# A decay-gated attention layer and a mixer MLP in one kernel: the recurrence, the loads and the order of all work rebuilt

## The chip, the core and the metric

One core of a Trainium2 chip runs the whole program. The metric is the device time of one execution in microseconds (us); lower is better. TensorE is called PE in the profile, VectorE DVE, ScalarE ACT, GpSimd POOL and SyncE SP.

## What is computed

Inputs: q, k, v, alpha of shape (4 batches, 8 heads, 768 steps, 48), float32, and the mixer's U (768 x 32), V (32 x 768), w_ch1 (384 x 1536), w_ch2 (1536 x 384). The output is (4, 768, 384) float32.

```python
state = np.zeros((B, H, D, D))
for t in range(S):
    state = alpha[:, :, t, :, None] * state + np.einsum('bhd,bhe->bhde', k[:, :, t], v[:, :, t])
    y[:, :, t] = np.einsum('bhd,bhde->bhe', q[:, :, t], state)
x = y.transpose(0, 2, 1, 3).reshape(B, S, H * D)
h = x.transpose(0, 2, 1) @ U @ V
u = x + h.transpose(0, 2, 1)
out = u + np.maximum(u @ w_ch1, 0.0) @ w_ch2
```

## The kernel before

A batch's 768 steps are cut into six chunks of 128; there are 24 chunks. `gla_chunk` does one. It loads alpha, q and k as float32 on the SP queue (lines 105 to 110; four buffers each) and v, cast to bf16 on its way, on the POOL queue (line 111). Ln of alpha (line 116) goes through two triangular matmuls: one gives the running sum from the chunk's start (line 119), one the sum from a step to the chunk's end (line 122). Three Exps turn these into `a_sb`, `ainv` and `arev` (lines 125 to 132). POOL makes q times `a_sb` (line 134) and k times `arev` (line 137), DVE makes k times `ainv` (line 135). PE transposes the q and k products, two heads at a time (lines 141 and 145), and DVE and ACT copy them to `qkT` (lines 150, 151). Scores of the even and odd heads (line 159) are masked by DVE (line 166). The chunk's y is the part from the state (line 173, two heads per matmul) plus the part from the scores (line 180), and ACT copies it to `x_b` (line 186). The state that a chunk hands on is made from its own k and v alone (line 191) and copied by DVE (lines 198, 199): decay over a whole chunk of 128 steps is so strong that what an older chunk leaves is dropped.

`moe_part(b, i)` is the mixer of a batch in six parts. Part 0 makes U^T x (line 208), V^T of that (line 216), u (line 220) and u transposed (lines 230, 242). Parts 1 and 2 are the MLP's first layer for one half of the steps each: 12 groups of three matmuls of 384 columns (line 251), with Relu on ACT and DVE in turn (lines 258, 262). Parts 3 to 5 are the second layer: 12 matmuls for each chunk (line 270), the add of u (line 277) and the store on the SP queue (line 278).

The order is that of the loop at the end: chunk c of batch b, then part c of the mixer of batch b - 1; the weights are sent on the POOL queue after the first chunk, 15 transfers with a cast to bf16, then U and V (lines 75 to 79). A scheduler of the language's library puts the engines' instructions in order and adds all waits. PSUM is eight banks: two for the sums, one for transposes, two and one for scores and state, and two (`pgen`) that y, the mixer and both MLP layers share.

Of the kernel before, what the change touches and what calls it, by code (L numbers as in the profile page):

```python
# [11 lines left out]
ALU = mybir.AluOpType  # L13


@with_exitstack
def kernel(
# [25 lines left out]
    xb_pool = ctx.enter_context(tc.tile_pool(name="xb_pool", bufs=2))
    io = ctx.enter_context(tc.tile_pool(name="io", bufs=4))
    work = ctx.enter_context(tc.tile_pool(name="work", bufs=4))
    moes = ctx.enter_context(tc.tile_pool(name="moes", bufs=2))
    outp = ctx.enter_context(tc.tile_pool(name="outp", bufs=4))

    pcum = ctx.enter_context(tc.tile_pool(name="pcum", bufs=2, space=bass.MemoryType.PSUM))
    ptp = ctx.enter_context(tc.tile_pool(name="ptp", bufs=1, space=bass.MemoryType.PSUM))  # L50
    ppts = ctx.enter_context(tc.tile_pool(name="ppts", bufs=2, space=bass.MemoryType.PSUM))
    ptodd = ctx.enter_context(tc.tile_pool(name="ptodd", bufs=1, space=bass.MemoryType.PSUM))
    pgen = ctx.enter_context(tc.tile_pool(name="pgen", bufs=2, space=bass.MemoryType.PSUM))

    def bank(pool, dtype=FP32, name="bk"):
        cols = 512 if dtype == FP32 else 1024
        return pool.tile([128, cols], dtype, name=name, tag="bk")
# [32 lines left out]
    ring_s = const.tile([128, 3, HP, 2 * D], BF16)  # L90
    nc.vector.memset(ring_s, 0.0)

    def pslice(ring, slot, p, wid=W):
        return ring[:, slot].rearrange("t h w -> t (h w)")[
            :, 2 * p * 64 : 2 * p * 64 + wid
        ]

    xs = [None] * B
    us = [None] * B

    def gla_chunk(b, c):
        x_b = xs[b]
        sl = slice(c * C, (c + 1) * C)
        slot = (b * NC + c) % RING
        at = io.tile([C, H, D], FP32, name="at")
        nc.sync.dma_start(at, alpha[b, :, sl, :].rearrange("h t d -> t h d"))
        qt = io.tile([C, H, D], FP32, name="qt")
        nc.sync.dma_start(qt, q[b, :, sl, :].rearrange("h t d -> t h d"))
        kt = io.tile([C, H, D], FP32, name="kt")
        nc.sync.dma_start(kt, k[b, :, sl, :].rearrange("h t d -> t h d"))  # L110
        nc.gpsimd.dma_start(  # L111
            ring_v[:, slot, :, 0:D], v[b, :, sl, :].rearrange("h t d -> t h d")
        )

        lt = work.tile([C, H * D], BF16, name="lt")
        nc.scalar.activation(lt, at.rearrange("t h d -> t (h d)"), AF.Ln)  # L116

        cum_ps = bank(pcum)[:, : H * D]
        nc.tensor.matmul(cum_ps, lhsT=ut_ones, rhs=lt, start=True, stop=True)  # L119
        if c < NC - 1:  # L120
            rev_ps = bank(pcum)[:, : H * D]
            nc.tensor.matmul(rev_ps, lhsT=sl_ones, rhs=lt, start=True, stop=True)

        a_sb = work.tile([C, H, D], BF16, name="a_sb")
        nc.scalar.activation(a_sb.rearrange("t h d -> t (h d)"), cum_ps, AF.Exp)  # L125
        ainv = work.tile([C, H, D], BF16, name="ainv")
        nc.scalar.activation(  # L127
            ainv.rearrange("t h d -> t (h d)"), cum_ps, AF.Exp, scale=-1.0
        )
        if c < NC - 1:  # L130
            arev = work.tile([C, H, D], BF16, name="arev")
            nc.scalar.activation(arev.rearrange("t h d -> t (h d)"), rev_ps, AF.Exp)  # L132

        nc.gpsimd.tensor_tensor(ring_q[:, slot, :, 0:D], qt, a_sb, op=ALU.mult)  # L134
        nc.vector.tensor_tensor(ring_k[:, slot, :, 0:D], kt, ainv, op=ALU.mult)  # L135
        if c < NC - 1:
            nc.gpsimd.tensor_tensor(ring_kh[:, slot, :, 0:D], kt, arev, op=ALU.mult)  # L137

        tp_ps = bank(ptp, BF16).rearrange("p (e c) -> p e c", c=C)
        for p in range(HP):  # L140
            nc.tensor.matmul(  # L141
                tp_ps[0:W, p, :], lhsT=pslice(ring_q, slot, p), rhs=ident,
                start=(p == 0), stop=False, is_transpose=True,
            )
            nc.tensor.matmul(  # L145
                tp_ps[0:W, HP + p, :], lhsT=pslice(ring_k, slot, p), rhs=ident,
                start=False, stop=(p == HP - 1), is_transpose=True,
            )
        qkT = work.tile([128, 8, C], BF16, name="qkT")
        nc.vector.tensor_copy(qkT[0:W, 0:HP], tp_ps[0:W, 0:HP])  # L150
        nc.scalar.copy(qkT[0:W, HP:], tp_ps[0:W, HP:])  # L151

        ptm = work.tile([C, H, C], BF16, name="ptm")
        pt_e = bank(ppts).rearrange("p (hp c) -> p hp c", c=C)
        pt_o = bank(ptodd).rearrange("p (hp c) -> p hp c", c=C)
        for par, pt_ps in ((0, pt_e), (1, pt_o)):
# [126 lines left out]
    for b in range(B + 1):  # L283
# [40 lines left out]
```

## Time and profile before

| | |
|---|---|
| median of 3 timed runs | 279.08 us (277.88 to 280.98) |
| span of the profiled execution, first to last instruction | 275.9 us |
| busy in it: PE / DVE / ACT / POOL | 197.0 / 132.0 / 137.1 / 75.1 us |
| mean granted clock of PE | 0.893 |
| read from HBM, written to HBM | 23.79 MB, 4.72 MB |

The profiled execution is told by its span; what lies around the span is seen only in the timed runs, whose median is 3.2 us above it. Busy time of PE has a modelled end for each matmul, so that overlapping matmuls are counted as one stretch and a single one is longer than its turn; the spacing of starts is the measure of a turn. An L and a number is a line of the kernel; `idle before` is how long the engine stood still ahead of a group, with what ended it.

### The profile page before, as it was taken

Reading aid. Unit: us, or ns where it says so; the run is one execution under the profiler, and the core shown is the slowest. Engines: PE = TensorE matmul, PEld = TensorE weight load, DVE = VectorE, ACT = ScalarE, POOL = GpSimd, SP = SyncE. Lnnn points to the kernel's source line nnn. Section 1 sums busy time; section 2 is a strip of 40 time slices with the busy share of each in tenths; the row PEclk is TensorE's granted clock in tenths of the full one; section 3 lists DMA queues with packets and bytes.
Section 4 is the critical chain, followed back from the end, with each engine's and each line's share of the span. In section 5 each row is a group of like instructions: output and inputs, shape, how many; then the busy total and the mean of one; then the engine's idle time right before and its main releaser. Section 6 shows DMA issues by size and latency. Waiting matters only on the chain.

```text
span 275.9 us, 3982 instructions
## 1 busy us (share of the span) xinstructions
PE 197.0 (71%) x1492; PEld 113.5 (41%) x1492; DVE 132.0 (48%) x247; ACT 137.1 (50%) x230; POOL 75.1 (27%) x99
## 2 busy tenths in 40 slices
PE   1440144856877878789627999987599998779995
PEld 0220023644244445445215556653455564344462
DVE  1330124664546545358515777458558644544421
ACT  3990789489889785555972553012034401014300
POOL 5736943564112034043101344242110000000000
PEclk9999999995557999999755999999579999959999
DMA  8999999999705594876502452435020011100022
GB/s 134 189 198 198 165 150 197 159 200 147 98 0 103 56 147 80 146 132 96 75 0 56 47 71 37 74 93 55 2 14 2 0 59 57 57 0 2 0 86 87
DMA packets 106306, 23.94 MB, mean 87 GB/s; under 512 B 101264, under 2 KB 105904, under 8 KB 106288
## 3 DMA queue, kind: packets, MB, share of 16 engines
q1 hardware_dynamic: 78336, 18.88, 32.2%
q0 software_dynamic: 27952, 4.82, 21.9%
q8 instruction: 11, 0.18, 0.2%
q14 instruction: 7, 0.06, 0.1%
HBM read 23.79 MB, written 4.72 MB: 103 GB/s over the span
## 4 chain that ended last, share of the span: by engine, by line
PE 50%; ACT 24%; issue 9%; DVE 8%; DMA 7%; SPq 1%; POOL 0%; ACTq 0%; DVEq 0%; POOLq 0%
PE bk L270 17%; PE bk L251 15%; DMA at<-in_alpha_dram 7%; ACT L116 5%; ACT L125 4%; PE bk L159 4%; ACT a_sb L125 3%; ACT ainv L127 2%; ACT lt L116 2%; ACT qkT L151 2%; PE bk L191 2%; PE bk L119 2%; ACT arev L132 2%; PE bk L141 2%; DVE h1t L262 2%
## 5 line engine op out<-in xcount | busy, mean ns | idle before, releaser
L251 PE MATMUL bk<-uT,w_sb 128*128 128x384 bf16 x288 | 61.4, 344 | 6.6 <-ACT h1t L258 3.7
L270 PE MATMUL bk<-w_sb,h1t 128*128 128x384 bf16 x288 | 51.3, 326 | 0.9 <-ACT x_b L186 0.4
L166 DVE TENSOR_TENSOR ptm<-bk,maskc 128x512 bf16<-128x512 f32 x48 | 31.5, 686 | 34.4 <-PE bk L159 33.9
L258 ACT ACTIVATE h1t<-bk 128x384 bf16<-128x384 f32 x48 | 23.6, 492 | 34.6 <-PE bk L251 32.7
L119 PE MATMUL bk<-lt,ut_ones 128*128 128x384 bf16 x24 | 10.3, 436 | 40.4 <-ACT lt L116 29.1
L251 PEld LDWEIGHTS <-w_sb 128*128 128x128 bf16 x288 | 27.8, 102 | 27.4 <-issue 14.1
L262 DVE TENSOR_SCALAR h1t<-bk 128x384 bf16<-128x384 f32 x48 | 26.7, 557 | 23.7 <-PE bk L251 23.0
L134 POOL TENSOR_TENSOR ring_q<-qt,a_sb 128x384 bf16<-128x384 f32 x24 | 22.4, 934 | 51.9 <-PE bk L145 23.1
L270 PEld LDWEIGHTS <-h1t 128*128 128x128 bf16 x288 | 26.8, 98 | 17.5 <-issue 1.2
L135 DVE TENSOR_TENSOR ring_k<-kt,ainv 128x384 bf16<-128x384 f32 x24 | 20.4, 855 | 25.0 <-ACT ainv L127 16.8
L111 POOL DMA_DIRECT2D ring_v<-in_v_dram x24 | 22.6, 941 | 28.6 <-PE bk L180 21.9
L137 POOL TENSOR_TENSOR ring_kh<-kt,arev 128x384 bf16<-128x384 f32 x20 | 18.6, 928 | 41.8 <-issue 20.0
L116 ACT ACT_TABLE_LOAD x19 | 24.4, 1283 | 9.2 <-DMA at<-in_alpha_dram 8.1
L277 DVE TENSOR_TENSOR out_sb<-u_b,bk 128x384 f32<-128x384 bf16 x24 | 13.3, 554 | 30.7 <-PE bk L270 30.7
L125 ACT ACT_TABLE_LOAD x17 | 21.8, 1283 | 10.8 <-PE bk L119 10.6
L186 ACT CAST x_b<-bk 128x384 bf16<-128x384 f32 x24 | 11.5, 479 | 29.0 <-PE bk L180 28.9
L151 ACT COPY qkT<-bk 112x512 bf16<-112x512 bf16 x24 | 14.1, 587 | 19.5 <-DVE qkT L150 19.2
L159 PE MATMUL bk<-qkT 48*128 48x128 bf16 x192 | 15.2, 252 | 9.0 <-ACT qkT L151 8.6
L141 PE MATMUL bk<-ident,ring_q 128*112 128x128 bf16 x96 | 19.1, 263 | 1.9 <-DVE uT L242 1.9
L145 PE MATMUL bk<-ident,ring_k 128*112 128x128 bf16 x96 | 19.3, 262 | 0.1
L141 PEld LDWEIGHTS <-ring_q 128*112 128x112 bf16 x96 | 15.6, 168 | 6.2 <-POOL ring_kh L137 4.6
L159 PEld LDWEIGHTS <-qkT 48*128 48x128 bf16 x192 | 8.0, 106 | 24.2 <-ACT qkT L151 18.1
(48 smaller groups left out, 230.9 us busy)
## 6 DMA issues: line engine op xcount, KB each, us to landing
at<-in_alpha_dram SPq DMA_DIRECT2D x24, 192.0 KB, 4.2
qt<-in_q_dram SPq DMA_DIRECT2D x24, 192.0 KB, 3.8
kt<-in_k_dram SPq DMA_DIRECT2D x24, 192.0 KB, 3.6
out_dram<-out_sb SPq DMA_DIRECT2D x24, 192.0 KB, 1.8
ring_v<-in_v_dram POOLq DMA_DIRECT2D x24, 96.0 KB, 3.8
w_sb<-in_moe_w_ch_dram POOLq DMA_DIRECT2D x3, 384.0 KB, 8.2
w_sb<-in_moe_w_ch_dram POOLq DMA_DIRECT2D x12, 96.0 KB, 7.2
u_sb<-in_moe_U_dram POOLq DMA_DIRECT2D x1, 48.0 KB, 6.7
```

Of the source, the lines that this page charges most:

```text
L111: nc.gpsimd.dma_start(ring_v[:, slot, :, 0:D], v[b, :, sl, :].rearrange("h t d -> t h d"))
L116: nc.scalar.activation(lt, at.rearrange("t h d -> t (h d)"), AF.Ln)
L125: nc.scalar.activation(a_sb.rearrange("t h d -> t (h d)"), cum_ps, AF.Exp)
L134: nc.gpsimd.tensor_tensor(ring_q[:, slot, :, 0:D], qt, a_sb, op=ALU.mult)
L135: nc.vector.tensor_tensor(ring_k[:, slot, :, 0:D], kt, ainv, op=ALU.mult)
L141: nc.tensor.matmul(tp_ps[0:W, p, :], lhsT=pslice(ring_q, slot, p), rhs=ident, start=(p == 0), stop=False, is_transpose=True,)
L159: nc.tensor.matmul(pt_ps[:, p, :], lhsT=qkT[o : o + D, HP + p, :], rhs=qkT[o : o + D, p, :], start=(p == 0), stop=(p == HP - 1),)
L166: nc.vector.tensor_tensor(ptv, pt_ps, maskc.to_broadcast([C, HP, C]), op=ALU.mult)
L251: nc.tensor.matmul(h1_ps, lhsT=w1_sb[:, ct, jt * 128 : (jt + 1) * 128], rhs=uT[:, ct, tt * TW : (tt + 1) * TW], start=(ct == 0), stop=(ct ...
L258: nc.scalar.activation(h1t[:, jt, tt * TW : (tt + 1) * TW], h1_ps, AF.Relu)
L262: nc.vector.tensor_scalar_max(h1t[:, jt, tt * TW : (tt + 1) * TW], h1_ps, 0.0)
L270: nc.tensor.matmul(ch_ps, lhsT=h1t[:, jt, c * C : (c + 1) * C], rhs=w2_sb[:, jt, :], start=(jt == 0), stop=(jt == NJ - 1),)
```

## The change

Both functions are rewritten, and all work is put into a list of operations with an engine, a cost in ns, what is read and written, and a priority. A planner in the kernel (`Plan`) walks through the list at build time: it keeps a clock for each engine and a line for the loads, takes always the operation that can start first, by priority where several can, gives it buffers and PSUM banks, and then emits everything in that order, which the library keeps (`manual_schedule`).

- All four inputs of a chunk are loaded as float32 on the SP queue, in the order alpha, k, q, v, into a ring of 40 tiles (ten chunks). POOL casts v to bf16.
- One sum from the chunk's start is left. Four matmuls with one column add the chunk's totals; a small Exp makes `tot` of them. The sum to the chunk's end, its Exp and the third product are gone.
- The state is kept in full: the old state is added through a matmul with the identity, k and v products of 48 columns are added to it, and DVE multiplies the sum by `tot`. The state part of y is one matmul of 48 rows per head.
- Both products are on POOL. The copies of u transposed move from DVE to ACT.
- The set of activation tables with Ln and Exp is named at the start.
- U and V (V four times) are sent after chunk 0, the first weight, as one transfer, after x of chunk 3, the second after x of chunk 4. U^T x is made in four strips of 32 rows.
- PSUM: two pairs of banks for scores and y, two banks for sums, transposes, state and mix, two for the MLP; the last batch's MLP takes any.
- Chunks have priority over the MLP, the mix over both.

The new code, cut to its core (the old code stands above):

```diff
+    LAT = {"PE": 230.0, "ACT": 120.0, "DVE": 120.0, "POOL": 150.0, "SP": 0.0, "DMA": 0.0}
...
+            for eng, cand in ready.items():
+                now = clock.get(eng, 0.0)
+                ok = []
+                for op in cand:
+                    t = op.est
+                    for b in op.bufs:
+                        if b.slot is None:
+                            s = [x for p in b.pools for x in p.free if x is not None]
+                            if not s:
+                                t = None
+                                break
+                            t = max(t, min(s))
+                    if t is not None:
+                        ok.append((max(t, now), op))
+                if not ok:
+                    continue
+                t0 = min(t for t, _ in ok)
+                t1, op = min(((t, o) for t, o in ok if t <= t0 + 1.0), key=lambda x: (x[1].prio, x[1].i))
+                if best is None or t1 < best[0]:
+                    best = (t1, eng, op)
...
+            if eng == "SP":
+                clock[eng] = t + 450.0
+                dma = max(dma, t + 450.0) + op.cost
+                op.end = dma + 1800.0
+            else:
+                clock[eng] = t + op.cost
+                op.end = t + op.cost
...
+        for _, op in order:
+            op.fn()
...
+def mm(*cols):
+    return sum(max(c, 54) / 2.4 + 2.5 for c in cols)
...
+    nc.scalar.preload_act_table_set("natural_log_exp_and_others")
...
+    io = Pool(slots("io", 40, [C, H, D], FP32))
...
+    outs = Pool(slots("ou", 4, [C, DM], FP32))
...
+    ps = psum.tile([128, 8, 512], FP32, name="ps")
+    pair = Pool([ps[:, 0:2, :], ps[:, 2:4, :]])
+    gen = Pool([ps[:, 4, :], ps[:, 5, :]])
+    mlp = Pool([ps[:, 6, :], ps[:, 7, :]])
...
+    def load_w1():
+        nc.gpsimd.dma_start(w1_sb, moe_w_ch1.rearrange("(c p) f -> p c f", p=128))
+    def load_w2():
+        nc.gpsimd.dma_start(w2_sb, moe_w_ch2.rearrange("(c p) f -> p c f", p=128))
...
+        at, qt, kt, vt = (Buf(io) for _ in range(4))
+        for t, src in ((at, alpha), (kt, k), (qt, q), (vt, v)):
+            P.add("SP", 960, lambda t=t, src=src: nc.sync.dma_start(t(), src[b, :, sl, :].rearrange("h t d -> t h d")), w=[t], prio=kk)
+        lt = Buf(lts)
+        P.add("ACT", 510, lambda: nc.scalar.activation(lt()[:, :, 0:D], at(), AF.Ln), r=[at], w=[lt], prio=pr + 4)
+        rv = Buf(rvs)
+        P.add("POOL", 500, lambda: nc.gpsimd.tensor_copy(rv(), vt()), r=[vt], w=[rv], prio=pr + 5)
...
+        def f_cum():
+            nc.tensor.matmul(cb()[:, 0:DM], lhsT=ut_ones, rhs=lt()[:, :, 0:D], start=True, stop=False)
+            for p in range(HP):
+                nc.tensor.matmul(
+                    cb()[:, DM + p : DM + p + 1],
+                    lhsT=lt()[:, 2 * p : 2 * p + 2, :].rearrange("t h w -> t (h w)"),
+                    rhs=ones, start=False, stop=(p == HP - 1),
+                )
+        P.add("PE", mm(DM, 1, 1, 1, 1), f_cum, r=[lt], w=[cb], prio=pr + 3, after=[done.get(kk - 2)])
...
+        P.add("ACT", 490, lambda: nc.scalar.activation(ai().rearrange("t h d -> t (h d)"), cb()[:, 0:DM], AF.Exp, scale=-1.0), r=[cb], w=[ai], prio=pr + 2)
+        P.add("ACT", 490, lambda: nc.scalar.activation(aa().rearrange("t h d -> t (h d)"), cb()[:, 0:DM], AF.Exp), r=[cb], w=[aa], prio=pr + 2)
+        P.add("ACT", 200, lambda: nc.scalar.activation(tot()[:, :, 0], cb()[:, DM : DM + HP], AF.Exp), r=[cb], w=[tot], prio=pr + 2)
...
+        P.add("POOL", 930, lambda: nc.gpsimd.tensor_tensor(rk()[:, :, 0:D], kt(), ai(), op=ALU.mult), r=[kt, ai], w=[rk], prio=pr + 2)
+        P.add("POOL", 930, lambda: nc.gpsimd.tensor_tensor(rq()[:, :, 0:D], qt(), aa(), op=ALU.mult), r=[qt, aa], w=[rq], prio=pr + 2)
...
+        P.add("PE", 220, lambda: f_tr(rk, HP), r=[rk], w=[(tb, "k")], prio=pr + 2, after=[done.get(kk - 2)])
+        P.add("PE", 220, lambda: f_tr(rq, 0), r=[rq], w=[(tb, "q")], prio=pr + 2)
+        P.add("ACT", 590, lambda: f_qk(HP, "ACT"), r=[(tb, "k"), (tb, "q")], w=[(qk, "k")], prio=pr + 1)
+        P.add("DVE", 410, lambda: f_qk(0, "DVE"), r=[(tb, "q"), (tb, "k")], w=[(qk, "q")], prio=pr + 1)
...
+        P.add("PE", mm(*[C] * 4) * 1.2, f_sc, r=[(qk, "k"), (qk, "q")], w=[sc], prio=pr + 1)
...
+            P.add("DVE", 690, lambda par=par: f_mask(par), r=[sc], w=[(pm, par)], prio=pr + 1)
...
+        def f_y(par):
+            y2 = yb()[:, par, 0 : HP * D].rearrange("p (hp d) -> p hp d", d=D)
             o = 64 * par
             for p in range(HP):
+                if sprev is not None:
+                    nc.tensor.matmul(
+                        y2[:, p, :], lhsT=qk()[o : o + D, p, :],
+                        rhs=sprev()[o : o + D, p, :], start=(p == 0), stop=False,
+                    )
             for p in range(HP):
                 nc.tensor.matmul(
+                    y2[:, p, :], lhsT=pm()[:, 2 * p + par, :], rhs=rv()[:, 2 * p + par, :],
+                    start=(p == 0 and sprev is None), stop=(p == HP - 1),
...
+            P.add("PE", mm(*[D] * 8), lambda par=par: f_y(par), r=rs + [(pm, par)], w=[(yb, par)], prio=pr)
...
+        P.add("ACT", 520, f_x, r=[(yb, 0), (yb, 1)], w=[(xb, c)], prio=pr)
...
+            def f_d():
+                d2 = db()[:, 0 : HP * D]
+                sp = sprev() if sprev is not None else s_zero
+                nc.tensor.matmul(d2[0:W], lhsT=ident[0:W, 0:W], rhs=sp[0:W].rearrange("p a d -> p (a d)"), start=True, stop=False, skip_group_check=True)
+                d3 = d2.rearrange("p (hp d) -> p hp d", d=D)
+                for p in range(HP):
+                    for par in range(2):
+                        o = 64 * par
+                        nc.tensor.matmul(
+                            d3[o : o + D, p, :], lhsT=rk()[:, 2 * p + par, 0:D], rhs=rv()[:, 2 * p + par, :],
+                            start=False, stop=(p == HP - 1), skip_group_check=True,
...
+            P.add("PE", mm(HP * D, *[D] * 8), f_d, r=[rk, rv] + ([sprev] if sprev is not None else []), w=[db], prio=pr + 1)
+            P.add(
+                "DVE", 340,
+                lambda: nc.vector.tensor_tensor(
+                    st()[0:W], db()[0:W, 0 : HP * D].rearrange("p (hp d) -> p hp d", d=D),
+                    tot()[0:W].to_broadcast([W, HP, D]), op=ALU.mult,
+                ),
+                r=[db, tot], w=[st], prio=pr,
...
+        P.add("PE", mm(DM) * 1.4, lambda: f_utx(range(0, 4)), r=[(xb, c) for c in range(4)] + ["u"], w=[xu], prio=pr)
+        P.add("PE", mm(DM) * 1.2, lambda: f_utx(range(4, NC)), r=[(xb, c) for c in range(4, NC)] + ["u"], w=[xu], prio=pr)
+        utx = Buf(utxs)
+        P.add("ACT", 490, lambda: nc.scalar.copy(utx(), xu()[:, 0:DM]), r=[xu], w=[utx], prio=pr)
...
+                P.add("ACT", 830, f_ev, r=[ub2], w=[(uT, c // 2)], prio=pr)
...
+        pool = [mlp] if b < B - 1 else [mlp, gen, pair]
...
+            if jt % 2 == 0:
+                P.add("ACT", 500, lambda jt=jt, hb=hb: nc.scalar.activation(h1()[:, jt, tt * TW : (tt + 1) * TW], bank(hb)[:, 0:TW], AF.Relu), r=[hb], w=[(h1, tt, jt)], prio=100)
+            else:
+                P.add("DVE", 560, lambda jt=jt, hb=hb: nc.vector.tensor_scalar_max(h1()[:, jt, tt * TW : (tt + 1) * TW], bank(hb)[:, 0:TW], 0.0), r=[hb], w=[(h1, tt, jt)], prio=100)
...
+        hb = Buf([mlp] if b < B - 1 else [mlp, gen, pair])
+        pr = 5000 + b * 1000 + 100 + (c % 3) * 33 + (0 if c < 3 else 100)
...
+            P.add("PE", mm(*[DM] * 4), f, r=[(h1, tt, jt) for jt in range(4 * g, 4 * g + 4)] + ["w2"], w=[hb], prio=pr + g)
+        ou = Buf(outs)
+        P.add("DVE", 550, lambda: nc.vector.tensor_tensor(ou(), ub()[:, c, :], bank(hb)[:, 0:DM], op=ALU.add), r=[hb, (ub, c)], w=[ou], prio=100)
+        P.add("SP", 550, lambda: nc.sync.dma_start(out[b, c * C : (c + 1) * C, :], ou()), r=[ou], prio=-1)
...
+            if b == 0 and c == 3:
+                x = P.ops[-1]
+                P.add("POOL", 1000, load_w1, r=[(xb, c)], w=["w1"], prio=0)
+            if b == 0 and c == 4:
+                P.add("POOL", 1000, load_w2, r=[(xb, c)], w=["w2"], prio=0)
...
```

## Rows read from the trace of the kernel before

**Rows 1.** The page: span, busy time of the engines, and the chain by engine.

```profile
span 275.9 us, 3982 instructions
...
PE 197.0 (71%) x1492; PEld 113.5 (41%) x1492; DVE 132.0 (48%) x247; ACT 137.1 (50%) x230; POOL 75.1 (27%) x99
...
PE 50%; ACT 24%; issue 9%; DVE 8%; DMA 7%; SPq 1%; POOL 0%; ACTq 0%; DVEq 0%; POOLq 0%
```

**Rows 2.** Busy time by stretch; the first line names the columns.

```profile
core 0: us, PE busy (x) PEld busy (x) DVE busy (x) ACT busy (x) POOL busy (x), PEclk, DMA share, GB/s
...
12.00:34.00 22.00, 4.50 (x30) 2.28 (x30) 3.56 (x7) 13.11 (x21) 15.34 (x24) 1.00 1.26 185
...
63.00:87.00 24.00, 17.84 (x118) 9.52 (x117) 12.08 (x25) 20.80 (x31) 5.03 (x7) 0.50 0.59 90
...
203.00:240.00 37.00, 34.04 (x283) 19.65 (x282) 20.42 (x40) 10.36 (x21) 0.94 (x1) 1.00 0.14 35
```

**Rows 3.** MLP matmuls: duration ns min/median/max, first and last start in us.

```profile
L251 PE MATMUL bk<-uT,w_sb x288: 322/326/528, 81.9 to 260.5; 128*128 128x384 bf16 x144
L270 PE MATMUL bk<-w_sb,h1t x288: 322/326/337, 109.0 to 272.2; 128*128 128x384 bf16 x144
```

**Rows 4.** Groups by line: busy us, mean ns, idle before and its releasers.

```profile
L116 ACT ACT_TABLE_LOAD x19 | 24.4, 1283 | 9.2 <-DMA at<-in_alpha_dram 8.1 <-PEq L308 0.8
...
L125 ACT ACT_TABLE_LOAD x17 | 21.8, 1283 | 10.8 <-PE bk L119 10.6
L134 POOL TENSOR_TENSOR ring_q<-qt,a_sb 128x384 bf16<-128x384 f32 x24 | 22.4, 934 | 51.9 <-PE bk L145 23.1 <-issue 14.6 <-ACT lt L116 5.2
...
L135 DVE TENSOR_TENSOR ring_k<-kt,ainv 128x384 bf16<-128x384 f32 x24 | 20.4, 855 | 25.0 <-ACT ainv L127 16.8 <-DMA kt<-in_k_dram 8.2
...
L151 ACT COPY qkT<-bk 112x512 bf16<-112x512 bf16 x24 | 14.1, 587 | 19.5 <-DVE qkT L150 19.2
...
L132 ACT ACTIVATE arev<-bk 128x384 bf16<-128x384 f32 x20 | 10.1, 505 | 1.2 <-PE bk L122 1.2
```

**Rows 5.** ACT in order of time: a table load and the Ln behind it.

```profile
33.84 1.28 ACT L116 ACT_TABLE_LOAD   x1
...
35.13 0.52 ACT L116 ACTIVATE lt<-at 128x384 bf16<-128x384 f32 x1
```

**Rows 6.** SP's queue while weights come in: first and last of six loads.

```profile
12.41 5.09 SPq L106 DMA_DIRECT2D at<-in_alpha_dram  x1
...
25.54 7.97 SPq L106 DMA_DIRECT2D at<-in_alpha_dram  x3
```

**Rows 7.** SP's queue without weights: first of nine loads, and the tenth.

```profile
40.42 0.65 SPq L110 DMA_DIRECT2D kt<-in_k_dram  x1
...
50.30 1.30 SPq L108 DMA_DIRECT2D qt<-in_q_dram  x1
```

**Rows 8.** PE in order of time, 202.9 to 208 us: start, length, what.

```profile
202.93 0.22 PE L145 MATMUL bk<-ident,ring_k 128*112 128x128 bf16 x1
202.98 0.22 PE L141 MATMUL bk<-ident,ring_q 128*112 128x128 bf16 x1
...
203.09 0.34 PE L180 MATMUL bk<-ring_v,ptm 128*128 128x48 bf16 x7
...
206.07 1.15 PE L251 MATMUL bk<-uT,w_sb 128*128 128x384 bf16 x6
207.16 0.34 PE L159 MATMUL bk<-qkT 48*128 48x128 bf16 x4
207.43 0.82 PE L251 MATMUL bk<-uT,w_sb 128*128 128x384 bf16 x4
```

**Rows 9.** PE at the end: two of the first layer's pairs of groups, then the second layer.

```profile
253.67 1.14 PE L251 MATMUL bk<-uT,w_sb 128*128 128x384 bf16 x6 [0.16 <-DVE h1t L262]
...
254.97 1.14 PE L251 MATMUL bk<-uT,w_sb 128*128 128x384 bf16 x6 [0.16 <-DVE h1t L262]
...
260.63 11.86 PE L270 MATMUL bk<-w_sb,h1t 128*128 128x384 bf16 x72
```

More of the change, by code (lines that the diff above doesn't have):

```diff
@@ L13, with __init__, __call__ @@
 ALU = mybir.AluOpType
+class Pool:
+    def __init__(self, slots):
+        self.slots = list(slots)
+        self.free = [0.0] * len(self.slots)
+class Buf:
+    def __init__(self, pool=None, slot=None):
+        self.pools = pool if isinstance(pool, list) else ([pool] if pool else [])
+        self.slot = slot
+        self.home = None
+        self.idx = 0
+        self.left = 0
+        self.last = 0.0
+    def __call__(self):
+        return self.slot
+class Op:
+    __slots__ = ("eng", "cost", "fn", "prio", "deps", "bufs", "n", "end", "users", "est", "i", "keep")
@@ L40 @@
     W = 112
+    TW = S // 2
     const = ctx.enter_context(tc.tile_pool(name="const", bufs=1))
[L43 to L57, printed above, removed]
@@ L71, with slots @@
-    vm_sb = const.tile([R, S], BF16)
+    psum = ctx.enter_context(tc.tile_pool(name="psum", bufs=1, space=bass.MemoryType.PSUM))
+    ctx.enter_context(tc.manual_schedule())
+    def slots(name, n, shape, dtype):
+        return [const.tile(shape, dtype, name=f"{name}{i}") for i in range(n)]
+    P = Plan()
+    nc.scalar.preload_act_table_set("natural_log_exp_and_others")
+    ut_ones = const.tile([C, C], BF16, name="ut_ones")
+    make_upper_triangular(nc, ut_ones, val=1.0, diag=True)
+    ident = const.tile([C, C], BF16, name="ident")
@@ L90 @@
[L90 to L102, printed above, removed]
-        sl = slice(c * C, (c + 1) * C)
[L104 to L143, printed above, removed]
-            )
[L145 to L156, printed above, removed]
@@ L270, in moe_part, with bank, mlp2, f @@
+    def bank(hb):
+        x = hb()
+        return x[:, 0, :] if len(x.shape) == 3 else x
+    def mlp2(b, ub, h1, c):
+        hb = Buf([mlp] if b < B - 1 else [mlp, gen, pair])
+        pr = 5000 + b * 1000 + 100 + (c % 3) * 33 + (0 if c < 3 else 100)
+        tt = c // 3
+        for g in range(3):
+            def f(g=g):
+                for jt in range(4 * g, 4 * g + 4):
                     nc.tensor.matmul(
-                        ch_ps,
-                        lhsT=h1t[:, jt, c * C : (c + 1) * C],
@@ L287 @@
+    for b in range(B):
+        xb, ub, uT, h1 = Buf(xbs), Buf(ubs), Buf(uts), Buf(h1s)
+        st = None
         for c in range(NC):
-            if b < B:
-                gla_chunk(b, c)
+            st = stage_gla(b, c, st, xb)
             if b == 0 and c == 0:
-                load_weights()
-            if b > 0:
-                moe_part(b - 1, c)
+                P.add("POOL", 1000, load_weights, w=["u", "vm"], prio=1000 + 25)
+            if b == 0 and c == 3:
[3 more added lines that the diff above has]
+                P.add("POOL", 1000, load_w2, r=[(xb, c)], w=["w2"], prio=0)
+        stage_mix(b, xb, ub, uT)
+        mlp1(b, uT, h1, 0)
+        mlp1(b, uT, h1, 1)
+        for c in range(NC):
+            mlp2(b, ub, h1, c)
```

341 lines of the change are left out of this document (208 added, 133 removed).

## The prediction

> **What bounds the kernel now.** I read the page first. Its totals [rows 1] show no engine that is full: PE, the busiest, is busy 197.0 us of the span of 275.9, and the chain that ended last is only half PE; a quarter of it is ACT and 7% is loads. So the time goes into waits between engines, and the question is where. The stretches [rows 2] say: from 12 to 34 us PE works 4.5 of 22 us while the DMA engines are full (share 1.26 by the profile's account); from 203 to 240 us PE is busy 34 of 37 us. The first and last starts of the MLP matmuls [rows 3] put a date to it: the first one starts at 81.9 us, the last at 272.2. The kernel is thus two parts: 82 us in which six chunks of attention are fetched and the mix is made, and 190 us in which PE does nearly all its matmuls. The groups [rows 4] show a reason for the slow first part and for holes in the second: 36 table loads of 1.28 us (19 before Ln, 17 before Exp) are 46.2 of ACT's 137.1 us, and they stand in the chain of every chunk.
>
> **PE's work, piece by piece, after the change.** At full clock a matmul of 384 columns follows the last one after 0.163 us (72 in 11.7 us, less the modelled end [rows 9]), one of 128 columns (a transpose) after 0.055, one of 48 columns after about 0.025 (seven in 0.34 us, of which some 0.18 is the last one's own latency) [rows 8].
> - MLP, unchanged: 576 x 0.163 = 93.7 us.
> - A chunk: running sum 0.16 and four one-column totals at 0.03; eight transposes 0.44; scores about 0.25; y sixteen of 48 columns 0.4; state one of 192 columns 0.08 and eight of 48 columns 0.2. Together 1.65 us.
> - A change of the array's shape: between two runs of full matmuls the four score matmuls with 48 rows cost more than their columns. Six matmuls from 206.07 should end their turn at 207.05, the scores start at 207.16; and they hold PE 0.27 us where four turns, two side by side, are 0.11 [rows 8]. So one visit costs about 0.2 us. A chunk now has four such visits (scores, two state parts of y, the state's 48-column strips): 0.75 us. The strips have no row of their own; between 0 and 0.2 I take 0.2, as the scores are the nearest.
> - Mix of a batch: six packed matmuls about 0.42, six of 384 columns 0.98, 18 transposes 1.0, visits 0.4: 2.8 us.
> The sum is 93.7 + 24 x 2.4 + 4 x 2.8 = 162.5 us, hardly other than before: the change saves PE no work. The Trainium skill (TensorEngine Tiling (Array Packing), Key Properties) says that a change of tiling mode, not of tile alone, drains TensorE; the scores' row agrees with it at 0.2 us, and by it the strips pay too; if they paid nothing the sum would be 24 x 0.2 = 5 us less.
>
> **When PE can begin.** In the stretch without weight transfers, nine loads of 192 KB go out between 40.42 and 50.30 us [rows 7], 1.1 us each, some v transfers of the other queue among them; I take 1.0 for a load alone. A chunk has now four of them on one queue: 4 us, six chunks 24, the first landing at about 3 us. While the weights came in before, six loads took 21 us (12.41 to 33.5 [rows 6]): the weights cost the loads about 15 us. Now they are sent after x of chunks 3 and 4, at about 25 and 29 us, so they delay chunk 5 little and the loads of the second batch much; with landing times of about 8 us and half of the engines, w1 is there at about 37 us. Chunk 5 lands at 28 to 30 us, x follows 5 us later (two multiplications of 0.93 on POOL, transposes, copies, masks, y), and the mix takes 6 us in its chain of copies. MLP starts at about 41 us instead of 81.9. Bounds: 35 (no delay by weights) and 60 (PE's fixed order has chunks 6 to 8 ahead of the first MLP groups, and their loads land behind the weights; the planner books the weights at 1 us of POOL and nothing on the DMA engines). In these 41 us PE gets seven chunks and a mix done: 7 x 2.4 + 2.8 = 19.6, so 143 us are left.
>
> **From there to the end.** Loads are 96 x 1.0 + 15 for weights, with stores perhaps 120 us, so the last chunk lands at about 120 us, when PE still has some 70 us of MLP to do: loads no longer bound the end, PE does. ACT loses the table loads and the third Exp (46.2 + 10.1), takes the uT copies (12 at about 0.9, from 0.587 for 512 columns [rows 4]) and 24 small Exp: about 95 us of work. DVE loses the k product (20.4): 112. POOL has two products of 0.93 and a cast of v of about 0.5 per chunk: 57. None reaches PE's 162. What PE loses to waits: MLP's first layer of batches 0 to 2 still has two PSUM banks, and where two banks alternated in the last stretch, six matmuls came every 1.30 us [rows 9] against 0.98 of their own. If nothing fills these holes they cost 36 pairs x 0.32 = 11.5 us; chunks, and the second layer's matmuls of the first half, lie beside some of it, so I take 7, no wait saved as the lower end, and as the upper end that PE's second part takes as long as before, 190 us. End of PE: 41 + 143 + 7 = 191. Behind the last matmul stand the add and the store, as before: 275.9 - 272.5 = 3.4. Span 194. The timed runs' median, 279.08, lies 3.2 above the profiled span, and I add as much: **197 us**. Its own range is 183 to 212.
>
> **Tables, by page and by row.** An Ln starts at 35.13 us, 0.01 after the load that began at 33.84 has ended [rows 5]: a switch costs 1.28 us. The Trainium skill (ScalarE: Activation LUTs, What ACT_TABLE_LOAD costs) says 1283 ns and about 1380 ns of drain, 2.66 us for every switch; the trace shows the first part and not the second. The same page (Table sets: the hidden batching unit) has Ln and Exp in one set, which no run here shows yet. By its 2.66 the 36 switches would be 96 us of ACT and not 46; what goes is off the path once PE bounds, so the sum stays.
>
> **Rivals.**
> 1. *The table loads stay* (the preload is not honoured). Then ACT has about 95 + 46 = 141 us, in the chunk phase 3.9 + 2.6 us per chunk: 18 chunks x 6.5 from 33 us end at 150, MLP of two batches and more is left, about 55 us. 150 + 55 + 3.4 + 3.2 = 212. For it: the choice of set is not the kernel's in what I see. Against: both functions can sit in one set.
> 2. *Fixed orders block.* Each engine works through the planner's order, and a late load, weight or store holds all behind it; stores go on the loads' queue behind loads sent far ahead, and only four output buffers exist. PE's second part then takes what it took before: 41 + 190 + 6.6 = 238; half of that loss gives 218.
> 3. *Better than summed*: MLP at 36 us, visits half price (-8), no holes: 36 + 135 + 6.6 = 177.
> 4. *The clock stays low: slower than before.* From 63 to 87 us the granted clock was 0.50, the 1.2 GHz level, though PE was busy 17.8 of 24 us; from 203 to 240 it was 1.00, the 2.4 GHz level, at 34 of 37 [rows 2]. If loads pace PE until 120 us and it is then cut by bank waits, it may stay at the lower level. All of the 143 us at that level gives 41 + 286 + 6.6 = 334; the sign turns when more than 0.55 of the work (79 us) runs there: 41 + 143 + 7 + 79 + 6.6 = 277. Against: MLP filled in leaves few holes.
>
> **How the numbers follow.** Forecast 0.64, rival 1 0.07, rival 2 0.14, rival 3 0.11, rival 4 0.04. The range, 173 to 226, holds rivals 1 and 3 and the milder half of 2; outside are its worse half, rival 4 and errors of a load's price. All but rival 4 and a sliver of 2 are faster by over 1%, which is about what can be told from no change: faster 0.95, same 0.01, slower 0.04.
>
> **What would show it.** Right: one table load; first MLP matmul at 36 to 48 us; loads full until about 120 us; PE's MLP spacing 0.163 and granted clock 1.00 from then on; chain mostly PE (70% or more). Wrong: MLP start beyond 60 us, DVE waiting for store buffers, table loads of more than two, PE idle over a tenth of the time between the first and the last MLP matmul, or the lower clock in more than a quarter of it.

## The result and the profile after

The kernel after takes 212.31 us (median of 4, 211.37 to 212.57) against 279.14 us (277.88 to 280.98): a ratio of 0.762, 95% interval 0.758 to 0.767. The forecast was 197, its range 173 to 226; the sign and the range hold, the time is 15 us longer than forecast. The profiled span is 210.8 us, 17 more than the forecast's 194. Of the runs below one (222.76 us, of e4) is in a slower state, which some executions of a kernel fall into, and its time is left out of the median.

The page of the kernel after: span, busy time, chain by engine, and its only group of table loads.

```profile
span 210.8 us, 4417 instructions
...
PE 174.7 (83%) x1732; PEld 107.5 (51%) x1732; DVE 97.4 (46%) x196; ACT 91.3 (43%) x209; POOL 60.8 (29%) x92
...
PE 57%; DMA 16%; SPq 14%; ACT 3%; issue 3%; DVE 3%; POOL 1%; POOLq 0%; ACTq 0%
...
L195 ACT ACT_TABLE_LOAD x1 | 1.3, 1283 | 0.7 <-PEq L515 0.7
```

Against [rows 1], ACT has gone from 24% of the chain to 3%, and DMA with the load queue from 8% to 30%. The 36 table loads of [rows 4] are one. (The Trainium skill, ScalarE: Activation LUTs, Table sets: the hidden batching unit, names a set that holds Ln and Exp together; one load for the whole run agrees.)

The MLP's two groups of matmuls, as in [rows 3]:

```profile
L447 PE MATMUL ps<-uT,w_sb x288: 322/326/524, 57.1 to 201.2; 128*128 128x384 bf16 x144
...
L471 PE MATMUL ps<-w_sb,h1t x288: 322/326/337, 69.6 to 207.0; 128*128 128x384 bf16 x144
```

The first starts at 57.1 us and not at 41; the last at 207.0. From first to last that is 150 us, and the forecast had 143 + 7. So the 16 us are lost before the MLP.

From the first MLP matmul's start to the last one's end, in the kernel before and in the kernel after (columns as in [rows 2]):

```profile
81.90:272.50 190.60, 159.25 (x1207) 90.69 (x1204) 100.76 (x189) 77.64 (x141) 32.54 (x35) 0.90 0.33 58
...
57.10:207.30 150.20, 144.57 (x1409) 87.53 (x1405) 79.34 (x155) 70.22 (x162) 37.27 (x49) 0.99 0.57 107
```

PE's idle time in it falls from 31.4 to 5.6 us and its busy time from 159.25 to 144.57, while the mean granted clock rises from 0.90 to 0.99. How much of the busy time is the clock's doing, no run separates.

The stretches show where the 16 us before the MLP are lost:

```profile
core 0: us, PE busy (x) PEld busy (x) DVE busy (x) ACT busy (x) POOL busy (x), PEclk, DMA share, GB/s
20.00:40.00 20.00, 14.58 (x171) 9.81 (x172) 7.50 (x14) 8.60 (x22) 10.37 (x13) 1.00 1.14 180
40.00:60.00 20.00, 8.97 (x78) 5.29 (x78) 5.82 (x12) 7.08 (x15) 3.12 (x5) 1.00 1.21 186
60.00:80.00 20.00, 19.71 (x250) 11.90 (x248) 12.09 (x25) 12.87 (x33) 9.70 (x14) 1.00 1.16 180
```

From 40 to 60 us PE has 8.97 us of work, and no other engine has more than 7.08; only the DMA engines are full. PE in order of time, around its longest idle time (in brackets: how long it waited, and for whom):

```profile
36.70 0.34 PE L352 MATMUL ps<-rv,pm 128*128 128x48 bf16 x4
...
38.02 0.50 PE L406 MATMUL ps<-xb,u_sb 128*32 128x384 bf16 x1
50.15 0.48 PE L406 MATMUL ps<-xb,u_sb 128*32 128x384 bf16 x1 [11.63 <-ACT xb L363]
```

This is the mix: its last U matmul waits for x of chunk 5, which ACT copies. ACT in order of time says why that copy was late:

```profile
36.70 0.18 ACT L284 ACTIVATE tot<-ps 128x4 f32<-128x4 f32 x1
49.21 0.52 ACT L265 ACTIVATE lt<-io 128x384 bf16<-128x384 f32 x1 [12.32 <-DMA io<-in_alpha_dram]
49.64 0.46 ACT L363 CAST xb<-ps 128x384 bf16<-128x384 f32 x1
```

y of chunk 5 (L352) was complete at about 37 us. ACT's fixed order has the Ln of chunk 7 ahead of the copy of x, and that Ln waits for its alpha. The chain of waits has the same load, from issue to landing:

```profile
30.76 18.43 DMA io<-in_alpha_dram
...
49.21 0.52 ACT lt L265
49.73 0.38 ACT xb L363
```

The median load of alpha lands 4.5 us after its issue; this one took 18.43. POOL's issues of the two weights, and SP's queue just behind them:

```profile
29.73 0.83 POOL L250 DMA_DIRECT2D w_sb<-in_moe_w_ch_dram  x1
...
32.12 1.09 POOL L253 DMA_DIRECT2D w_sb<-in_moe_w_ch_dram  x1
```

```profile
31.80 8.73 SPq L263 DMA_DIRECT2D io<-in_k_dram  x1
40.57 4.86 SPq L263 DMA_DIRECT2D io<-in_q_dram  x1
45.48 3.55 SPq L263 DMA_DIRECT2D io<-in_v_dram  x1
```

The DMA view of 38 to 46 us: packets, MB, and share of the 16 engines by queue (software: the weights; hardware: the loads).

```profile
q0 software_dynamic: 1417, 1.22, 93.5%
q1 hardware_dynamic: 1415, 0.27, 30.7%
```

Both queues move the same number of packets, but the weights' hold some 860 bytes on average and the loads' 192: the loads get 0.27 MB where eight undisturbed microseconds (50 to 58) give 1.58. The Trainium skill (DMA: Bandwidth & Descriptors, Queues, rings and completion order) says that each DMA engine goes round-robin between its queues by whole packets; 1417 to 1415 agrees, if what the trace counts is the page's packet, which no run here shows.

A second, smaller loss: DVE writes the first out tile at 72.0 us, SP issues the first store at 106.5 us, behind loads sent ahead, and the four out buffers run out. DVE's group, SP's first store, and PE's largest wait between 57 and 208 us:

```profile
L478 DVE TENSOR_TENSOR ou<-ub,ps 128x384 f32<-128x384 bf16 x24 | 13.3, 553 | 30.8 <-PE ps L471 27.8 <-DMA out_dram<-ou 2.7
...
106.51 1.17 SPq L479 DMA_DIRECT2D out_dram<-ou  x1
...
PE ps L417 <- DVE ou L478: 2.4, 2, 2.0
```

So the theory to be tested (theory W): the weights' transfer makes the alpha of chunk 7 late, and the order written before the run lets that hold x of chunk 5, the mix and the MLP. Its rivals: stores behind loads cost the 15 us (S); or every load is dearer, 19.4 ns for a packet of 192 bytes against 16.3 in the kernel before (means over each trace), and the loads are late with or without weights (L).

### The profile page after: what moved, and what is told of

It reads as the page before. It is cut to its first block, busy times and chain, and to the rows that moved or that the text cites. A ratio compares the mean times of both kernels' runs of the same rounds, so it can differ in the third digit from the quotient of the medians.

```text
span 210.8 us, 4417 instructions
## 1 busy us (share of the span) xinstructions
PE 174.7 (83%) x1732; PEld 107.5 (51%) x1732; DVE 97.4 (46%) x196; ACT 91.3 (43%) x209; POOL 60.8 (29%) x92
## 4 chain that ended last, share of the span: by engine, by line
PE 57%; DMA 16%; SPq 14%; ACT 3%; issue 3%; DVE 3%; POOL 1%; POOLq 0%; ACTq 0%
PE ps L471 21%; PE ps L447 20%; SPq L263 14%; DMA io<-in_alpha_dram 11%; DMA io<-in_v_dram 4%; PE ps L295 3%; PE ps L321 3%; PE ps L352 2%; PE ps L347 2%; DMA out_dram<-ou 2%; PE ps L427 2%; PE ps L417 2%; DVE ub L418 1%; PE ps L381 1%; PE ps L272 1%
## 5 line engine op out<-in xcount | busy, mean ns | idle before, releaser
L447 PE MATMUL ps<-uT,w_sb 128*128 128x384 bf16 x288 | 54.9, 329 | 0.5 <-ACT h1t L455 0.4
L471 PE MATMUL ps<-w_sb,h1t 128*128 128x384 bf16 x288 | 51.9, 326 | 0.0
L455 ACT ACTIVATE h1t<-ps 128x384 bf16<-128x384 f32 x48 | 23.4, 491 | 38.7 <-PE ps L447 38.6
L332 DVE TENSOR_TENSOR pm<-ps,maskc 128x512 bf16<-128x512 f32 x48 | 31.5, 685 | 18.8 <-PE ps L321 18.7
L457 DVE TENSOR_SCALAR h1t<-ps 128x384 bf16<-128x384 f32 x48 | 26.2, 555 | 16.6 <-PE ps L447 16.0
L286 POOL TENSOR_TENSOR rk<-io,ai 128x384 bf16<-128x384 f32 x24 | 21.9, 913 | 37.6 <-ACT ai L282 35.2
L478 DVE TENSOR_TENSOR ou<-ub,ps 128x384 f32<-128x384 bf16 x24 | 13.3, 553 | 30.8 <-PE ps L471 27.8
L287 POOL TENSOR_TENSOR rq<-io,aa 128x384 bf16<-128x384 f32 x24 | 21.9, 911 | 0.5 <-ACT tot L284 0.3
L304 ACT COPY qk<-ps 128x512 bf16<-128x512 bf16 x24 | 14.0, 583 | 13.0 <-PE ps L295 8.6
L321 PE MATMUL ps<-qk 48*128 48x128 bf16 x192 | 11.2, 247 | 5.3 <-ACT qk L304 3.4
L352 PE MATMUL ps<-rv,pm 128*128 128x48 bf16 x192 | 13.8, 193 | 1.1 <-DVE pm L332 1.0
L406 PE MATMUL ps<-xb,u_sb 128*32 128x384 bf16 x24 | 3.6, 376 | 12.8 <-ACT xb L363 11.6
L295 PEld LDWEIGHTS <-rq 128*128 128x128 bf16 x96 | 7.1, 108 | 13.6 <-issue 12.4
```

The costliest lines, as they stand in the source:

```text
L286: P.add("POOL", 930, lambda: nc.gpsimd.tensor_tensor(rk()[:, :, 0:D], kt(), ai(), op=ALU.mult), r=[kt, ai], w=[rk], prio=pr + 2)
L287: P.add("POOL", 930, lambda: nc.gpsimd.tensor_tensor(rq()[:, :, 0:D], qt(), aa(), op=ALU.mult), r=[qt, aa], w=[rq], prio=pr + 2)
L304: nc.scalar.copy(qk()[:, o : o + HP, :], t[:, o : o + HP, :])
L321: nc.tensor.matmul(s2[:, par, p, :], lhsT=qk()[o : o + D, HP + p, :], rhs=qk()[o : o + D, p, :], start=(p == 0), stop=(p == HP - 1),)
L332: nc.vector.tensor_tensor(pm().rearrange("t (hp two) c -> t two hp c", two=2)[:, par], s2[:, par], maskc.to_broadcast([C, HP, C]), op=ALU. ...
L352: nc.tensor.matmul(y2[:, p, :], lhsT=pm()[:, 2 * p + par, :], rhs=rv()[:, 2 * p + par, :], start=(p == 0 and sprev is None), stop=(p == HP ...
```

## The experiments

Medians are of 4 runs each (3 for e4); a ratio is to the kernel before (0.762 for the kernel after).

**No weight transfer (e1, e1b).**

```diff
-        nc.gpsimd.dma_start(w1_sb, moe_w_ch1.rearrange("(c p) f -> p c f", p=128))
+        nc.gpsimd.memset(w1_sb[:, 0, 0:DM], 0.01)
...
+    nc.vector.memset(w1_sb, 0.01)
+    nc.vector.memset(w2_sb, 0.01)
```

(the same for w2; in e1b the last two lines are 24 short planned instructions instead)

> Leaves out the transfer of both MLP weight matrices (they are filled with a constant in the kernel), so the output's MLP part is another. Theory W (the weights' transfer takes the DMA engines from about 32 to 47 us, the alpha of chunk 7 lands late, and ACT's fixed order holds x of chunk 5 and with it the mix behind its logarithm): the gap of 12 us in PE before the second U matmul goes, the first MLP matmul starts at 40 to 43 us, the time is 195 to 199 us. Rival S (stores behind loads and four out buffers cost the 15 us): MLP may start earlier, but the time stays at 206 us or more. Rival L (each load is dearer, 19.4 ns against 16.3 ns a packet, and chunks 6 to 8 are late anyway): first MLP matmul at 50 us or later.

199.32 us, ratio 0.717 (0.713 to 0.721); first MLP matmul at 48.4, not 40 to 43, since the two long fills, 3.9 us each, kept DVE from the zeroing that the first chunk needs. Hence:

> As e1_no_weight_transfer, with the constant filled in by 24 short DVE instructions instead of two long ones, because the long ones held the first chunk's scores back by 5.9 us (PE's first transposes at 12.48 us, 6.62 us in the kernel after). It leaves out the transfer of the MLP weights. Theory W, freed of that: first MLP matmul at 41 to 44 us and 192 to 196 us in all, that is, the forecast's 197 us or less. If e1's 12.7 us were all that the transfer costs, the time stays at 198 to 200 us.

200.66 us, 0.720 (0.714 to 0.725). The MLP group and the stretch of 40 to 60 us:

```profile
L447 PE MATMUL ps<-uT,w_sb x288: 322/326/527, 45.5 to 189.7; 128*128 128x384 bf16 x144
...
40.00:60.00 20.00, 19.28 (x224) 12.14 (x223) 12.71 (x26) 14.34 (x34) 9.01 (x12) 1.00 1.26 185
```

PE is full where it had 8.97 us. The MLP starts 11.6 us earlier and the time falls by 11.65 us (by 13.0 in e1): the transfer costs 12 to 13 us. That start and time agree so closely in e1b is partly luck, for e1 starts its MLP 2.9 us later than e1b and is 1.3 us faster. DVE waits 1.0 us for a store in e1b and not in e1, and e1b's granted clock is low for 6.8 us, while e1's record has no low stretch:

```profile
98.60:105.50 6.90, 5.74 (x52) 3.33 (x48) 2.76 (x5) 2.98 (x8) 2.39 (x4) 0.51 1.06 204
```

S and L fall as explanations of the whole, though a load's packet takes 19.4 ns in e1b too; but W was too hopeful: 41 to 44 and 192 to 196 were expected. x of chunk 5 is there at 38 us even without weights, some 3 us later than the prediction had it (33 to 35), and the mix takes 7.2 us and not 6.

**ACT's order alone (e2).** `mixed` holds the mix's last uT copy.

```diff
-AF.Ln), r=[at], w=[lt], prio=pr + 4)
+AF.Ln), r=[at], w=[lt], prio=pr + 4, after=mixed if kk in (7, 8) else ())
...
+        mixed.append(P.ops[-1])
```

> Keeps every transfer; only the plan is told that the logarithms of chunks 7 and 8 come behind the mix of the first batch, so ACT's order has x of chunk 5, the U copy and the uT copies ahead of them. Theory W: the 12 us gap in PE shrinks to what v of chunk 6 (converted at 44.6 us in the kernel after) and then alpha of chunk 7 (49.2 us) still hold, so the first MLP matmul comes at 45 to 47 us, some 12 MLP matmuls run ahead of the wait for chunk 7, and the time falls by 6 to 11 us, to 201 to 206 us. Rivals S and L: the order of ACT costs nothing that loads or stores don't cost anyway, less than 3 us gained.

210.17 us, 0.756 (0.750 to 0.761): 2 us instead of 6 to 11. PE in order of time:

```profile
45.12 1.14 PE L449 MATMUL ps<-uT,w_sb 128*128 128x384 bf16 x6
...
52.70 0.32 PE L273 MATMUL ps<-lt,ut_ones 128*128 128x384 bf16 x1 [1.98 <-ACT lt L266]
...
61.12 0.36 PE L382 MATMUL ps<-rv,rk 128*48 128x48 bf16 x8 [5.77 <-POOL rk L287]
```

The MLP starts at 45.1, as expected. But the loads are as late as in the kernel after, PE's order has chunks 7 to 9 between MLP groups, and PE waits before each; 40 to 60 us holds 10.27 us of PE work, and the granted clock is then 0.50 from 53.8 to 64.1. The late start of the MLP is not the cause by itself: the order of chunks 7 to 9 is wrong as well for loads that come this late, and mending one place hands the wait to the next.

**Twelve out buffers (e3).** `slots("ou", 4, ...)` becomes `slots("ou", 12, ...)`.

> Twelve out buffers instead of four, nothing else in the program is edited. Rival S: DVE and PE no longer wait for stores behind the loads (2.7 and 2.0 us seen there), and the time falls by 10 us or more. Theory W: the first MLP matmul stays at 57 us, the waits at 117 to 121 us go, the time falls by 2 to 4 us, to 208 to 210 us.

207.80 us, 0.747 (0.742 to 0.752): 4.5 us less, first MLP matmul still at 56.5. PE's wait for the out tile falls from 2.4 us to

```profile
PE ps L417 <- DVE ou L478: 0.3, 1, 0.3
```

S is real, and is 4.5 us of the 15.

**A ring of 16 load tiles (e6).** `slots("io", 40, ...)` becomes `slots("io", 16, ...)`.

> The ring of load tiles cut from 40 to 16, nothing else edited (the plan is made anew for it). If the loads are paced by their own 1.0 us and a ring of four chunks keeps the queue full until about 122 us as one of ten does, the time stays within 3 us of the kernel after. If the depth is what keeps loads running while the MLP has PE, loads end later than 130 us and the time rises by 5 to 15 us.

206.79 us, 0.742 (0.738 to 0.747): faster by 5.5, which neither case had. Loads end at 118.5 us as with 40 tiles, and the MLP starts at 56.3. But SP can't run so far ahead of use, and its first store goes out 27.6 us earlier:

```profile
78.87 0.94 SPq L479 DMA_DIRECT2D out_dram<-ou  x1
```

The loads did not need ten chunks of ring, and the stores were kept waiting by it. It is the gain of e3 by another way: the 2.7 us that DVE waits for stores in the kernel after are gone in both.

**The tables (e4 and b1).** e4 is the kernel after without its `preload_act_table_set` line; b1 is the kernel before with that line.

> The line that loads one activation table at the start is taken out, nothing else. If one table for logarithm and exponential is a large part of the change, table loads of 1.28 us come back at each turn from logarithm to exponential (some 40 of them, 50 us of ACT, which is then at 140 us of busy time) and the time rises by 15 to 40 us. If ACT's slack hides them (ACT is idle for 120 of 211 us), the time rises by less than 8 us; either way the tables are charged in the first 57 us, where ACT stands on the path, at 1.28 us each for some 14.

218.92 us, 0.789 (0.782 to 0.797): 6.6 us more by the medians, 7.6 by the ratios. The table loads are back:

```profile
L264 ACT ACT_TABLE_LOAD x17 | 21.8, 1283 | 1.0 <-PEq L514 0.7
L281 ACT ACT_TABLE_LOAD x17 | 21.8, 1283 | 3.1 <-PE ps L273 2.2 <-issue 0.7
```

43.6 us of ACT cost some 7 us: the new order hides most of them.

> The kernel before with one part of the change alone: the activation table that holds logarithm and exponential is loaded at the start. The 39 or so table loads of 1.28 us leave ACT (some 48 us of its time). If they stood on the path throughout, the time falls by 40 us or more, to 240 or less; if PE's fewer and better ordered instructions are the larger part of the gain of 67 us, it falls by 10 to 25 us, to 255 to 270; if ACT's loads were hidden, by less than 5.

250.83 us, 0.901 (0.893 to 0.908): 28.7 us less, between the expected cases. In the old order the table loads stood in the chain; b1's MLP now starts at 71.5 us instead of 81.9 [rows 3] and its last matmul at 245.5 instead of 272.2:

```profile
L252 PE MATMUL bk<-uT,w_sb x288: 322/326/528, 71.5 to 233.8; 128*128 128x384 bf16 x144
L271 PE MATMUL bk<-w_sb,h1t x288: 322/326/337, 92.2 to 245.5; 128*128 128x384 bf16 x144
```

So one line gives 43% of the gain of 67 us, though what it is worth depends on the order around it.

**Program order instead of the list schedule (e9).**

```diff
+                    if eng != "SP" and op is not queue[eng][0]:
+                        continue
```

> The instructions of the kernel after with the list schedule's choice taken out on PE, ACT, DVE and POOL: each of these engines gets its work in the order in which the program adds it (chunk by chunk, then the mix, then the MLP of the same batch); the load queue's order is still planned. If the list schedule is a main part of the gain, PE waits inside each chunk with no MLP work beside it (24 chunks of 6 to 8 us, four mixes of 6, four MLP parts of 23.4): 250 to 310 us. If the rebuilt arithmetic alone carries the gain and the order little: 215 to 230 us.

337.82 us, ratio 1.212 (1.202 to 1.221), 28 us above the expected range and slower than the kernel before. PE's first transposes of the first three chunks:

```profile
8.46 0.61 PE L301 MATMUL ps<-ident,rk 128*128 128x128 bf16 x4 [3.48 <-POOL rk L292]
...
16.57 0.61 PE L301 MATMUL ps<-ident,rk 128*128 128x128 bf16 x4 [1.57 <-POOL rk L292]
...
24.66 0.61 PE L301 MATMUL ps<-ident,rk 128*128 128x128 bf16 x4 [1.62 <-POOL rk L292]
```

A chunk takes 8.1 us when nothing is laid beside it, and in three stretches of 51.2 us each the granted clock is 0.50. In this order the new arithmetic is slower than the kernel before, and against it the list schedule is worth 125 us, low clock included. It is not the old order: the kernel before lays a part of a batch's mixer behind each chunk of the next batch, and e9 lays nothing there. The new arithmetic in the old order was not run, so what the arithmetic is worth by itself stays open.

**Weights on the loads' queue (e7), with twelve out buffers (e8).**

```diff
-                P.add("POOL", 1000, load_w1, r=[(xb, c)], w=["w1"], prio=0)
...
-                P.add("POOL", 1000, load_w2, r=[(xb, c)], w=["w2"], prio=0)
...
+            P.add("SP", 550, lambda wt=wt, src=src: nc.sync.dma_start(wt().rearrange("p h d -> p (h d)"), src), w=[wt], prio=5.5)
+            P.add("POOL", 500, lambda wt=wt, dst=dst: nc.gpsimd.tensor_copy(dst, wt().rearrange("p h d -> p (h d)")), r=[wt], w=[("W1", i)] if i < NJ else [("W2", i)], prio=1055 + 0.1 * i)
```

> The MLP weights are loaded in 24 pieces of 192 KB in fp32 on the loads' own queue, between the loads of chunk 5 and chunk 6, through the ring of load tiles, and POOL converts each (24 of about 0.5 us). No transfer competes with chunks 0 to 5, and the plan knows when the weights and the later chunks come. Theory W: no gap of 12 us in PE, first MLP matmul at 40 to 46 us, MLP of the first batch runs while the later chunks load; 198 to 203 us. If what costs is the transfer's bytes and not the order (loads until 120 us either way), the wait only moves: 208 us or more.

> As e7_weights_sp, and twelve out buffers. The two gains add if they are different waits: 4 us below e7_weights_sp, 194 to 199 us. If the store wait only shows because the MLP started late, it equals e7_weights_sp within 1.5 us.

e7: 207.78 us, 0.745 (0.740 to 0.750); e8: 198.01 us, 0.710 (0.706 to 0.715), 14.3 us below the kernel after. Both start the MLP at 43 us, as W expected, but e7 misses its 198 to 203, and e8 lies 9.8 below it, not 4. The MLP's second layer (L478) in two stretches of e7 (columns: length, PE busy and PEld busy on this line, granted clock, DMA share, GB/s):

```profile
82.00:88.00 6.00, 0.66 (x4) 0.20 (x2) 1.00 1.29 190
88.00:97.00 9.00, 0.00 (x0) 0.00 (x0) 0.50 1.16 200
```

and the first layer (L454) of e8 in the second of them:

```profile
88.00:97.00 9.00, 4.72 (x24) 1.99 (x24) 1.00 1.25 198
```

With four out buffers the plan of e7 has no MLP matmul between about 83 and 107 us, only chunks and a mix: PE is busy 3.73 of the 6 us before 88, and from 88.0 the clock is 0.50 for 27.3 us. In e8 the clock falls nowhere before 195.7. That the lower clock makes the 5 us beyond e3's gain is argued from these rows and not shown; there is no run with e7's order at the full clock.

The MLP group of e8:

```profile
L454 PE MATMUL ps<-uT,w_sb x288: 322/326/337, 43.2 to 186.4; 128*128 128x384 bf16 x144
```

**Two tries beyond e8 (e11, e12).** e11 adds 50 matmuls of zeros in PE's early idle places; e12 sends the weights behind chunk 6's loads (`prio=6.5`).

> As e8_weights_sp_out12 (with eleven out buffers instead of twelve) and 50 matmuls of zeros, 384 columns each, that the plan puts into PE's idle places before the first mix. In all kernels of this design a 128x384 matmul takes 0.48 to 0.51 us in the first 42 to 55 us and 0.32 to 0.34 us later, though the granted clock of that stretch is shown as 1.00. If the early chunks are held by PE's slower rows, more work before them brings the shorter rows earlier and the first MLP matmul from 43.2 to 38 to 41 us: 193 to 196 us. If they are held by loads and the other engines, nothing or the matmuls' own time is seen: 198 to 203 us.

> As e8_weights_sp_out12, with the 24 weight loads behind chunk 6's loads instead of chunk 5's, so that the plan can lay chunk 6's work into PE's idle places before 43 us (some 5 us in 20 to 40 us there). If those places can hold it and the weights are still there when the mix ends, the time falls by 1 to 3 us, to 195 to 197 us. If the mix or the weights' conversion on POOL is held back by as much, it stays at 197 to 200 us.

e11: 199.40 us, 0.716 (0.712 to 0.721); e12: 198.00, 0.715 (0.708 to 0.721): neither gains. Two stretches of e11:

```profile
19.10:26.00 6.90, 6.26 (x97) 3.95 (x95) 3.54 (x8) 3.82 (x10) 2.99 (x5) 1.00 1.05 184
...
32.70:43.00 10.30, 7.50 (x60) 4.70 (x61) 4.53 (x9) 2.42 (x5) 10.19 (x22) 0.50 1.03 348
```

The running sum's matmul takes 0.33 us from 21 to 29 us (0.48 in e8), yet the MLP starts at 44.1, 0.9 us later than in e8. Up to 31 us e11's chain of waits is load issues and landings, and PE does not pace the chunks. From 33 us the chain runs through PE's work for chunk 5 and the mix, and there the clock is down again; so what short rows would be worth in that part e11 does not tell. In e12 PE does more from 20 to 40 us (16.75 us of work against 15.05 in e8), and the MLP starts 1.1 us later.

## Why the prediction was right, and where it was off

- *Where the kernel is bound, and the sign*: right. Before, 82 us of fetching and 190 of PE; after, 57 and 150. PE is the chain's largest part from the MLP's start.
- *PE's second part, 143 + 7*: right, 150. But the 7 is met by luck. The prediction had PE wait for the MLP's two banks; it stands 5.6 us idle in 57 to 207 us, of which 0.6 are waits for h1 or its copy, 2.4 for the out buffer and most of the rest for operands of the chunks and the mix, and 3.4 us of its work run at the low clock.
- *A visit at 0.2 us, a chunk at 2.4*: near, but the parts are not. In the chain's view of the kernel after, at a granted clock of 1.00, a piece lasts until the next one starts:

```profile
100.35 0.20 PE ps L347 x4
100.55 0.20 PE ps L352 x4
100.75 0.11 PE ps L376
100.86 0.21 PE ps L381 x8
101.07 0.55 PE ps L295 x8
...
103.33 0.33 PE ps L321 x8
```

  With 0.24 us for the running sum and the totals, and y's two lines (L347, L352) twice, a chunk is 2.24 us. The scores (L321) take 0.33 where 0.25 and a visit of 0.2 were summed. The state's eight strips (L381) take 0.21, their columns' price alone, so the 0.2 us taken for their visit is not seen; the transposes (L295) take 0.55 and not 0.44.
- *Loads 1.0 us each and 15 for the weights, ending at about 120*: right; the last load is issued at 118.5, and the weights hold up the load queue from 32 to 49 us.
- *Tail 3.4*: 3.5. *Span to median 3.2*: 1.5. In each execution with both figures the time is 1.6 to 2.2 us above its span (212.57 and 210.8 for the profiled one); the 3.2 set a median beside the span of another, faster execution.
- *MLP starts at about 41 us*: this step failed, at 57.1, and it is the miss. Bounds of 35 and 60 were given, and what was said for 60 is what came: fixed orders have later chunks ahead, their loads land behind the weights, and the planner books nothing on the DMA engines. The sum took 41 because the weights "delay chunk 5 little", which was true of its loads. But it was not the loads of chunk 5 that held the mix: the Ln of chunk 7 did, one place ahead in ACT's order, with its alpha 18.43 us on the way. 11.65 us go with the transfer (e1b), and 41 was itself 4.5 short of what is seen without it (45.5).
- *Rival 2, fixed orders block*: it had the right mechanism for both losses, store queue and out buffers included (4.5 us in e3). It stood among the rivals at 0.14, and nothing of it was in the sum. With both losses mended and the weights loaded another way, e8 takes 198.01 us, against the 197 that was forecast for the kernel after.
- *Rival 1*: one table load, so no. Had they stayed, the price is some 7 us (e4) and not the 15 of this rival.
- *Rival 4, the low clock*: 3.4 us of the kernel after. In e7 and e9 it came where chunks ran with no MLP between them (27.3 us, and three times 51.2).
- *The signs*: of those for being right, one table load, loads until about 120 us and the spacing of 0.163 (72 matmuls in 11.70 us, the clock at 1.00 but for 3.4 us) came; the MLP's start (57.1, not 36 to 48) and the chain (PE 57%, not 70%) did not. Of those for being wrong one came: DVE waited 2.7 us for store buffers.

## What to carry to other kernels

An order fixed before the run is as good as its model of the slowest resource: here the list schedule is worth 125 us against the program's own order, and one transfer booked at nothing on the DMA engines costs 12 to 13. When you read such a planner, look for transfers that its clock doesn't know, find which operations stand just ahead of the critical one in each engine's order, and price the miss by what they wait for. A deep load ring can cost if stores share its queue: 40 load tiles were 5.5 us slower here than 16.

## What the runs showed of the hardware that was not expected

Two queues shared the DMA engines by packets and not by bytes: 1417 to 1415 packets in 8 us, 1.22 to 0.27 MB. Two transfers of 1152 KB with big packets thus stretched the landing of a 192 KB load of small ones from 4.5 to 18.4 us.

The granted clock reads 1.00 from the start of each trace, but rows of one kind differ: in the kernel after, a single matmul of 384 columns takes 0.48 to 0.53 us until 50 us and 0.32 to 0.33 us from 56.8 us on where the clock is recorded as 1.00, and the trace's first record of the clock is at 54.8 us. The same matmul takes 0.50 to 0.53 us in e7 from 93 to 98 us, where the clock is recorded as 0.50. So the early rows are those of the 1.2 GHz level, whatever the column says; only rows tell. In e11, with zeros from the start, the first record is at 5.4 us and the short rows come early; the clock is at 0.50 from 12.3 to 19.1 us, and falls again at 32.7 us, after a stretch (26.0 to 32.7) in which PE was busy 3.71 of 6.7 us.
